# Totals of 31 heads moved from between two VectorE products to behind both, in a decode attention kernel

## The chip, the cores and the metric

The kernel runs on one core of a Trainium2 chip. The metric is device time in microseconds (us), the median of several executions. A profile is one execution recorded by the hardware profiler; its span is about 1.8 us shorter than the device time of the same execution.

Engine names in the profile: PE is TensorE (matmuls), PEld its weight loads, DVE is VectorE, ACT is ScalarE, SP is SyncE, which issues the transfers (DMA).

## The reference

Cut to what matters: one query of 32 heads attends to a cache of 65,536 keys and values per head. A small gated feed-forward part and a sigmoid gate are mixed in.

```
q      = (x @ wq) as 32 heads of 128
scores = q . k_cache / sqrt(128)          # 32 x 65536
p      = softmax(scores)
o      = p . v_cache
a      = o @ wo
b      = (silu(x @ w_gate) * (x @ w_up)) @ w_down
out    = g * a + (1 - g) * b              # g = sigmoid(sum(x * gate_w))
```

The caches are 1.07 GB in bf16, each byte read once. The softmax's division is put off: the kernel forms unnormalised sums, keeps the row sums of the exponentials, and divides at the end by the *totals*.

## The kernel before

A head is two *chunks* of 32,768 keys, so there are 64 chunks, 0 to 63. Three buffers (slots) of the same size hold keys and values in turn. For each chunk VectorE multiplies the keys by the query in place (*product*, two halves per chunk), TensorE sums over each key's 128 elements by matmuls with an identity matrix (*sums*), VectorE finishes the sum (*gather*), ScalarE makes the exponential, and TensorE multiplies by the values (*value product*, 64 matmuls).

```python
def norm(h0, h1):                       # totals
    mms("tot_ps", m_x[...], [(ones, rowsum[:, ...])], ...)       # TensorE
    dve("tot",   ... tensor_reduce(out=tot[:, h0:h1], in_=m_x ...))
    dve("recip", ... reciprocal(tot[:, h0:h1]))

def outputs():                          # normalised outputs of heads 0..30
    dve("oT", ... oT = o_all * tot)

for n in range(N - 1):                  # chunks 0..62
    ...                                 # load keys and values of chunk n
    m = HK if n else EK
    for j in range(0, KPP, m):          # two halves
        block(n, j, m)                  # product on VectorE, sums on TensorE
        if j == 0:
            if c == 0 and h + 1 < H:
                spread(h + 1)
            if pending:
                diagonal()              # TensorE, then ScalarE: last output of a head
            if n == N - 2:              # chunk 62: all of heads 0..30 is done
                norm(0, H - 1)
                outputs()
        while len(todo) > 1:
            gather()
    gather()
    ...
    if n == N - 2:
        turn_outputs(0)                 # t_ps: oT turned by TensorE
    pv(n)                               # value product

# chunk 63, cut: in four quarters, with the last weights
load("v", n, V_END)                     # last values, five pieces
turn_outputs(1)
for i, j in enumerate(range(0, KPP, EK)):
    block(n, j, EK)                     # short product, short sums
    if i == 0:
        rows("b_ps", ...)               # 56 one-column matmuls
        diagonal()
    if i == 1:
        dve("rest", ...)
        rows("a_ps", ...)               # 128 one-column matmuls
    ...
```

The order in which the program issues these calls is the order in which each engine runs them in the profiles: in the kernel before, TensorE runs the first sums of chunk 62 at 2448.51 us, the diagonal at 2457.33 and tot_ps at 2458.30, as issued.

The softmax here doesn't subtract the row's maximum and nothing guards it: scores larger than these inputs give would overflow.

Of the kernel before, what the change touches and what calls it, by code (L numbers as in the profile page):

```python
# [79 lines left out]
def kernel(  # L80
# [18 lines left out]
    _, H, Sk, Dh = A_k_cache.shape  # L99
# [8 lines left out]
    N = H * CH  # L108
# [89 lines left out]
    def load(which, n, pieces):  # L198
        cache = A_k_cache if which == "k" else A_v_cache
        h, c = divmod(n, CH)  # L200
        s = where[which, n] = take()
        src = cache[0, h, c * P * KPP : (c + 1) * P * KPP, :].rearrange(
            "(p j) d -> p j d", j=KPP
        )
        t = view(s, 0, KPP, Dh)
        at = 0
        for m in pieces:
            dma(
                (which, n, at), t[:, at : at + m, :], src[:, at : at + m, :],
                units(s, at * Dh, (at + m) * Dh),  # L210
                sem=f"slot{s}" if len(pieces) == 1 else f"{which}{n}_{at}",
            )
            at += m
        assert at == KPP
# [31 lines left out]
    def mms(key, out_ap, pairs, reads, writes, start=True, stop=True):  # L246


        def fn():
            for i, (a, b) in enumerate(pairs):  # L250
                ins = nc.tensor.matmul(  # L251
                    out_ap, lhsT=a, rhs=b,
                    start=start and i == 0, stop=stop and i == len(pairs) - 1,
                )
            return ins

        op("PE", key, fn, reads, writes)
# [20 lines left out]
    def dve(key, fn, reads, writes):  # L278
        op("DVE", key, fn, reads, writes)
# [26 lines left out]
    def spread(h):  # L306

        act("dq", dq, ident, ACT.Copy, ["ident", "qT"], ["dq"], scale=qT[:, h : h + 1])
        mms("spread", m_sp[:, :Dh], [(ones_b, dq)], ["ones_b", "dq"], ["m_sp"])
        q = h % 2  # L310
        act("q_bc", q_bc[q], m_sp[:, :Dh], ACT.Copy, ["m_sp"], [("q_bc", q)])
# [4 lines left out]
    def block(n, j, m):  # L316

        s, h = where["k", n], n // CH
        qb = q_bc[h % 2]
        q_rep = bass.AP(tensor=qb.tensor, offset=qb.offset, ap=[list(qb.ap[0]), [0, m], [1, Dh]])  # L320
        w = view(s, 0, KPP, Dh)[:, j : j + m, :]
        names = units(s, j * Dh, (j + m) * Dh)
        dve(
            "products", lambda: nc.vector.tensor_tensor(out=w, in0=w, in1=q_rep, op=ALU.mult),  # L324
            names + [("q_bc", h % 2)], names,
        )
        r = ring["S"] % 2
        ring["S"] += 1
        B = 512 // R
        group(  # L330
            ("sums", s, j, m, r),
            [
                (
                    S_ps[r][:, b : b + B, :],
                    [(ident, w[:, b : b + B, i * R : (i + 1) * R]) for i in range(Dh // R)],
                )
                for b in range(0, m, B)
            ],
            names + ["ident"], [("S_ps", r)],
        )  # L340
        todo.append((n, j, m, r))

    def gather():
        n, j, m, r = todo.pop(0)
        b = ring["Sb"] % 2
        ring["Sb"] += 1
        dve(
            "gather",
            lambda: nc.vector.tensor_reduce(  # L349
                out=S_sb[b][:, :m], in_=S_ps[r][:, :m, :], axis=AXIS.X, op=ALU.add  # L350
            ),
            [("S_ps", r)], [("S_sb", b)],
        )
        col = n * RS + j // EK
        act(
            "exp", P_sb[n % 2][:, j : j + m], S_sb[b][:, :m], ACT.Exp,
            [("S_sb", b), "rowsum"], [("P_sb", n % 2, u) for u in range(j // EK, (j + m) // EK)]
            + [("rowsum", col)],
            scale=scale, accum_out=rowsum[:, col : col + 1],
        )  # L360
# [25 lines left out]
    def diagonal():  # L386

        h = pending.pop(0)
        mms(
            ("diagonal", h == H - 1), m_c[:, 0:1],  # L390
            [(O_sb[:, j * Dh : (j + 1) * Dh], pick[:, j : j + 1]) for j in range(VB)],
            ["O_sb", "pick"], ["m_c"], stop=(h < H - 1),
        )
        if h < H - 1:
            act("o_all", o_all[:, h : h + 1], m_c[:, 0:1], ACT.Copy, ["m_c"], [("o_all", h)])

    def hidden():
        parts = []
        for w, wv in enumerate((gate_v, up_v)):
            for ft in range(FT):  # L400
                parts.append(
                    (
                        m_x[:, w * FT + ft : w * FT + ft + 1],
                        [(wv[:, t, bass.ds(ft, P, FT)], Xc[:, t : t + 1]) for t in range(KT)],
                    )
                )
        group("gu", parts, units(0, G0, U0 + KT * F) + ["Xc"], ["m_x"])
        act("gu_sb", gu_sb, m_x[:, : 2 * FT], ACT.Copy, ["m_x"], ["gu_sb"])
        act("eg", eg, gu_sb[:, :FT], ACT.Exp, ["gu_sb"], ["eg"], scale=-1.0)
        dve("eg1", lambda: nc.vector.tensor_scalar_add(eg, eg, 1.0), ["eg"], ["eg"])  # L410
        dve("eg2", lambda: nc.vector.reciprocal(eg, eg), ["eg"], ["eg"])
        dve(
            "eg3",
            lambda: nc.vector.tensor_tensor(out=eg, in0=gu_sb[:, :FT], in1=eg, op=ALU.mult),
            ["eg", "gu_sb"], ["eg"],
        )
        dve(
            "hT",
            lambda: nc.vector.tensor_tensor(out=hT, in0=eg, in1=gu_sb[:, FT:], op=ALU.mult),
            ["eg", "gu_sb"], ["hT"],  # L420
        )

    def gate():
        dve(
            "s_t",
            lambda: nc.vector.tensor_tensor_reduce(
                out=xg, in0=x_row, in1=gw_row, scale=1.0, scalar=0.0,
                op0=ALU.mult, op1=ALU.add, accum_out=s_t,
            ),
            ["x_row", "gw_row"], ["xg", "s_t"],  # L430
        )
        mms("s_ps", m_x[:, 0:1], [(ones[0:1, :], s_t)], ["ones", "s_t"], ["m_x"])
        act("gexp", gval, m_x[:, 0:1], ACT.Exp, ["m_x"], ["gval"], scale=-1.0)
        dve("g1", lambda: nc.vector.tensor_scalar_add(gval, gval, 1.0), ["gval"], ["gval"])
        dve("g2", lambda: nc.vector.reciprocal(gval, gval), ["gval"], ["gval"])
        dve(
            "g3",
            lambda: nc.vector.tensor_scalar(
                out=ngval, in0=gval, scalar1=-1.0, scalar2=1.0, op0=ALU.mult, op1=ALU.add
            ),  # L440
            ["gval"], ["ngval"],
        )
# [15 lines left out]
    def norm(h0, h1):  # L458
        w = CH * RS
        mms("tot_ps", m_x[:, : (h1 - h0) * w], [(ones, rowsum[:, h0 * w : h1 * w])],  # L460
            ["ones", "rowsum"] + [("rowsum", i) for i in range(h0 * w, h1 * w)], ["m_x"])
        dve(
            "tot",
            lambda: nc.vector.tensor_reduce(
                out=tot[:, h0:h1],
                in_=m_x[:, : (h1 - h0) * w].rearrange("p (h c) -> p h c", c=w),
                axis=AXIS.X, op=ALU.add,
            ),
            ["m_x"], [("tot", h0)],
        )  # L470
        dve("recip", lambda: nc.vector.reciprocal(out=tot[:, h0:h1], in_=tot[:, h0:h1]),
            [("tot", h0)], [("tot", h0)])

    def outputs():

        dve(
            "oT",
            lambda: nc.vector.tensor_tensor(
                out=oT[:, : H - 1], in0=o_all[:, : H - 1], in1=tot[:, : H - 1], op=ALU.mult
            ),  # L480
            [("o_all", h) for h in range(H - 1)] + [("tot", 0)], ["oT"],
        )
# [18 lines left out]
    for n in range(N - 1):  # L501
        h, c = divmod(n, CH)
        if c == 0:
            cut[h] = len(plan.ops)
        if n:
            load("k", n, [KPP])
            load("v", n, [KPP])
        m = HK if n else EK
        for j in range(0, KPP, m):
            block(n, j, m)  # L510
            if j == 0:
                if c == 0 and h + 1 < H:
                    spread(h + 1)
                if pending:
                    diagonal()
                if n == N - 2:
                    norm(0, H - 1)
                    outputs()
            while len(todo) > 1:
                gather()  # L520
        gather()
        if n == 0:
            gate()
            hidden()
        if n == N - 2:
            turn_outputs(0)
        pv(n)


    n, h = N - 1, H - 1  # L530
# [132 lines left out]
```

## Time and profile before

| | before |
|---|---|
| median of the first three executions | 2534.17 us (2532.98 to 2534.49) |
| span of the profile | 2530.3 us |
| transfers, share of 16 engines' span | 99.3% |
| VectorE, TensorE busy | 50%, 78% |

The page says what bounds the kernel as a whole. The first line of the fence is the span, the second the mean busy share of the DMA engines in 40 slices of the span (tenths, 9 is 90% or more), the third the queue of the caches (packets, MB, share of 16 engines).

```profile
span 2530.3 us, 19415 instructions
...
DMA  9999999999999999999999999999999999999996
...
q1 hardware_dynamic: 20880, 1087.78, 99.3%
```

Only the last slice is short of full, and the queue is at 99.3% of the span. So in this kernel an engine's wait should cost nothing while it holds up no transfer; that leaves the end. The change sits there, in chunk 62.

This is VectorE's timeline in chunk 62: start, length, the instruction, and in brackets the idle time before it and what ended it.

```profile
2439.76 8.69 DVE L324 TENSOR_TENSOR slot_67<-slot_67,q_bc_79 128x16384 bf16<-128x16384 bf16 x1 [12.39 <-DMA slot_67<-in_A_k_cache_dram]
2458.96 0.42 DVE L464 TENSOR_REDUCE tot<-m_x 128x31 f32<-128x248 f32 x1 [10.50 <-PE m_x L251]
2459.41 0.35 DVE L471 RECIPROCAL tot<-tot 128x31 f32<-128x31 f32 x1
2459.86 0.20 DVE L478 TENSOR_TENSOR oT<-o_all,tot 128x31 bf16<-128x31 f32 x1
2459.97 8.68 DVE L324 TENSOR_TENSOR slot_67<-slot_67,q_bc_79 128x16384 bf16<-128x16384 bf16 x1
```

The first product (8.69 us) starts when the keys land at 2439.76. Then VectorE stands idle 10.50 us for one TensorE result, tot_ps in `m_x`, works 0.97 us on totals, and only then starts the second product. The keys of the second product came with those of the first. Why tot_ps comes late is seen in the chain of waits (the work that ended last, followed back; start, length, engine and what it writes: `S_ps` are sums, `m_c` with x8 the diagonal, `m_x` at x2 tot_ps and at x56 a group of one-column matmuls called b_ps, `O_ps` the value product).

```profile
2448.51 8.81 PE S_ps_101 L265 x32
2457.33 0.98 PE m_c L251 x8
2458.30 0.63 PE m_x L251 x2
...
2460.06 8.61 DVE slot_67 L324
...
2468.71 8.97 PE S_ps_102 L265 x32
...
2479.41 13.97 PE O_ps L251 x64
...
2493.58 3.56 PE S_ps_101 L265 x16
2497.14 1.83 PE m_x L265 x56
2498.97 0.98 PE m_c L251 x8
2499.95 5.21 PE S_ps_102 L265 x16
```

tot_ps (`m_x` at 2458.30) stands on TensorE behind the first sums (8.81 us) and the diagonal (0.98 us). From the value product at 2479.41 on, the chain is TensorE without a gap until its last products. Two short sums of equal work take 3.56 and 5.21 us. That difference is the clock (1.00 during the first; 0.59 on average over 2500 to 2504 us). Groups at half clock are called *cold*, stretches at half clock *slow spells*.

Last, the transfers at the end: windows of 2 us, with TensorE's granted clock (1.00 is full speed, 0.50 half), the DMA share and GB/s as the last three columns.

```profile
2490.00:2492.00 2.00, 2.00 (x11) 0.82 (x10) 0.00 (x0) 0.00 (x0) 0.00 (x0) 1.00 0.31 131
2492.00:2494.00 2.00, 2.00 (x14) 0.77 (x13) 0.00 (x0) 0.57 (x2) 0.00 (x0) 1.00 0.00 0
2494.00:2496.00 2.00, 2.00 (x11) 0.94 (x10) 0.00 (x0) 0.09 (x2) 0.00 (x0) 1.00 0.87 262
```

There is a hole in the transfers: the last values need the slot that the value product of chunk 62 reads, so they are issued only when it ends, at 2493.42.

### The profile page before, as it was taken

How to read it: one execution, taken by the hardware profiler on the slowest of the kernel's cores; microseconds unless marked ns; L12 is line 12 of the kernel's file. 1: busy time of each engine (PE TensorE's matmuls, PEld its weight loads, DVE VectorE, ACT ScalarE, POOL GpSimd, SP SyncE). 2: the span in 40 equal slices, each digit the busy share in tenths (PEclk: the TensorE clock that was granted, in tenths of full speed). 3: DMA queues.
4: the chain of work that ended last, by engine and by line, in shares of the span. 5: the costliest groups of instructions: out<-in, count | busy, mean ns of one | idle time of the engine just before them, and what ended most of it. 6: DMA issues, size and time to landing. Idle time of an engine off the chain costs nothing.

```text
span 2530.3 us, 19415 instructions
## 1 busy us (share of the span) xinstructions
PE 1981.2 (78%) x9115; PEld 823.6 (33%) x9115; DVE 1268.3 (50%) x286; ACT 97.4 (4%) x398; POOL 1.9 (0%) x9
## 2 busy tenths in 40 slices
PE   4787877877877878778778778787787787787868
PEld 2233332333333333323333333333333233333324
DVE  3455355464464554554644645545546446455453
ACT  0000000000000000000000000000000000000000
POOL 0000000000000000000000000000000000000000
PEclk8888988989889889889989898898898998988988
DMA  9999999999999999999999999999999999999996
GB/s 421 432 433 433 435 434 434 434 432 436 434 434 435 431 437 433 435 435 431 436 433 436 435 431 435 434 434 436 432 435 434 433 436 433 435 433 434 434 430 289
DMA packets 20906, 1088.09 MB, mean 430 GB/s; under 512 B 2450, under 2 KB 2580, under 8 KB 2836
## 3 DMA queue, kind: packets, MB, share of 16 engines
q1 hardware_dynamic: 20880, 1087.78, 99.3%
q8 instruction: 16, 0.26, 0.0%
q14 instruction: 6, 0.05, 0.0%
q10 hardware_dynamic: 4, 0.00, 0.0%
HBM read 1087.77 MB, written 0.00 MB: 430 GB/s over the span
## 4 chain that ended last, share of the span: by engine, by line
DMA 44%; PE 41%; DVE 13%; ACT 1%; another core or an unknown queue 0%; issue 0%; SPq 0%; DVEq 0%; ACTq 0%
PE O_ps L251 18%; DMA slot_67<-in_A_k_cache_dram 16%; DMA slot_66<-in_A_k_cache_dram 14%; DMA slot_65<-in_A_k_cache_dram 14%; PE S_ps_101 L265 12%; PE S_ps_102 L265 9%; DVE slot_67 L324 4%; DVE slot_66 L324 4%; DVE slot_65 L324 3%; DVE S_sb_82 L349 2%; PE m_c L251 1%; PE m_x L265 1%; ACT P_sb_83 L274 1%; DMA slot_65<-in_A_wq_dram 0%
## 5 line engine op out<-in xcount | busy, mean ns | idle before, releaser
L265 PE MATMUL S_ps_101<-slot_67,ident 128*128 128x512 bf16 x704 | 204.6, 462 | 133.7 <-DVE slot_67 L324 133.7
L265 PE MATMUL S_ps_101<-slot_66,ident 128*128 128x512 bf16 x672 | 195.5, 463 | 127.9 <-DVE slot_66 L324 127.9
L265 PE MATMUL S_ps_101<-slot_65,ident 128*128 128x512 bf16 x672 | 190.1, 453 | 133.8 <-DVE slot_65 L324 133.8
L349 DVE TENSOR_REDUCE S_sb_82<-S_ps_102 128x128 f32<-128x1024 f32 (+1 forms) x66 | 78.7, 1192 | 396.9 <-PE S_ps_102 L265 396.9
L324 DVE TENSOR_TENSOR slot_67<-slot_67,q_bc_79 128x16384 bf16<-128x16384 bf16 (+1 forms) x26 | 207.9, 8031 | 133.1 <-DMA slot_67<-in_A_k_cache_dram 133.1
L324 DVE TENSOR_TENSOR slot_65<-slot_65,q_bc_78 128x16384 bf16<-128x16384 bf16 x22 | 190.2, 8689 | 146.5 <-DMA slot_65<-in_A_k_cache_dram 146.5
L324 DVE TENSOR_TENSOR slot_66<-slot_66,q_bc_78 128x16384 bf16<-128x16384 bf16 (+1 forms) x24 | 190.6, 7977 | 136.9 <-DMA slot_66<-in_A_k_cache_dram 121.2
L324 DVE TENSOR_TENSOR slot_67<-slot_67,q_bc_78 128x16384 bf16<-128x16384 bf16 x20 | 172.9, 8688 | 120.6 <-DMA slot_67<-in_A_k_cache_dram 120.6
L324 DVE TENSOR_TENSOR slot_65<-slot_65,q_bc_79 128x16384 bf16<-128x16384 bf16 x20 | 172.9, 8688 | 119.1 <-DMA slot_65<-in_A_k_cache_dram 119.1
L324 DVE TENSOR_TENSOR slot_66<-slot_66,q_bc_79 128x16384 bf16<-128x16384 bf16 x20 | 172.9, 8689 | 117.7 <-DMA slot_66<-in_A_k_cache_dram 117.7
L251 PE MATMUL O_ps<-slot_67,P_sb_83 128*4 128x512 bf16 x704 | 155.6, 382 | 28.5 <-ACT P_sb_83 L274 18.3
L251 PE MATMUL O_ps<-slot_65,P_sb_83 128*4 128x512 bf16 x704 | 153.7, 379 | 19.9 <-ACT P_sb_83 L274 19.9
L251 PE MATMUL O_ps<-slot_66,P_sb_84 128*4 128x512 bf16 x704 | 153.7, 379 | 19.3 <-ACT P_sb_84 L274 19.3
L265 PE MATMUL S_ps_102<-slot_67,ident 128*128 128x512 bf16 x704 | 159.4, 385 | 9.9 <-DVE slot_67 L324 9.8
L265 PEld LDWEIGHTS S_ps_101<-slot_67,ident 128*128 128x128 bf16 x704 | 79.0, 115 | 258.7 <-DVE slot_67 L324 144.3
L265 PEld LDWEIGHTS S_ps_101<-slot_66,ident 128*128 128x128 bf16 x672 | 75.7, 115 | 247.7 <-DVE slot_66 L324 138.7
L265 PEld LDWEIGHTS S_ps_101<-slot_65,ident 128*128 128x128 bf16 x672 | 74.3, 113 | 249.9 <-DVE slot_65 L324 144.4
L251 PE MATMUL O_ps<-slot_67,P_sb_84 128*4 128x512 bf16 x640 | 139.7, 379 | 18.3 <-ACT P_sb_84 L274 18.3
L251 PE MATMUL O_ps<-slot_65,P_sb_84 128*4 128x512 bf16 x640 | 139.7, 379 | 18.3 <-ACT P_sb_84 L274 18.3
L251 PE MATMUL O_ps<-slot_66,P_sb_83 128*4 128x512 bf16 x640 | 139.7, 379 | 17.5 <-ACT P_sb_83 L274 17.5
L265 PE MATMUL S_ps_102<-slot_66,ident 128*128 128x512 bf16 x672 | 148.8, 379 | 1.3 <-DVE slot_66 L324 1.3
L265 PE MATMUL S_ps_102<-slot_65,ident 128*128 128x512 bf16 x672 | 148.6, 379 | 0.3 <-DVE slot_65 L324 0.2
(83 smaller groups left out, 860.6 us busy)
## 6 DMA issues: line engine op xcount, KB each, us to landing
slot_66<-in_A_k_cache_dram SPq DMA_DIRECT2D x4, 2048.0 KB, 24.9
slot_67<-in_A_k_cache_dram SPq DMA_DIRECT2D x4, 2048.0 KB, 17.8
slot_65<-in_A_wq_dram SPq DMA_DIRECT2D x1, 4096.0 KB, 12.4
slot_66<-in_A_wo_dram SPq DMA_DIRECT2D x1, 4096.0 KB, 30.8
slot_65<-in_A_v_cache_dram SPq DMA_DIRECT2D x1, 4096.0 KB, 13.3
slot_65<-in_A_v_cache_dram SPq DMA_DIRECT2D x1, 2048.0 KB, 17.8
slot_65<-in_B_w_gate_dram SPq DMA_DIRECT2D x1, 1792.0 KB, 35.0
slot_65<-in_B_w_up_dram SPq DMA_DIRECT2D x1, 1792.0 KB, 38.8
```

The costliest lines, as they stand in the source:

```text
L251: ins = nc.tensor.matmul(out_ap, lhsT=a, rhs=b, start=start and i == 0, stop=stop and i == len(pairs) - 1,)
L265: ins = nc.tensor.matmul(out_ap, lhsT=a, rhs=b, start=(i == 0), stop=(i == len(pairs) - 1))
L274: "ACT", key, lambda: nc.scalar.activation(out=out_ap, in_=in_ap, func=func, **kw),
L324: "products", lambda: nc.vector.tensor_tensor(out=w, in0=w, in1=q_rep, op=ALU.mult),
L349: lambda: nc.vector.tensor_reduce(out=S_sb[b][:, :m], in_=S_ps[r][:, :m, :], axis=AXIS.X, op=ALU.add),
```

## The change

The intent is to let the two products of chunk 62 follow each other as in every other chunk. The totals are issued behind the second half's product and sums instead of between the halves.

```diff
                 if pending:
                     diagonal()
-                if n == N - 2:
-                    norm(0, H - 1)
-                    outputs()
+            elif n == N - 2:
+                norm(0, H - 1)
+                outputs()
             while len(todo) > 1:
                 gather()
```

No instruction is added or removed. On TensorE, tot_ps moves behind the second sums; on VectorE, three small instructions move behind the second product, ahead of the two gathers.

## The prediction

> **What bounds the kernel now.** DMA, almost everywhere: 430 GB/s over the span, 99% of 16 engines (page, parts 2 and 3). A chunk of keys and values takes 38.6 us, which the transfers fill, so the change can only act at the end. There (windows of 4 us) the DMA share is about 1.0 until 2488 us, falls to 0.59 and 0.43 in 2488-2496, and is full again until 2513. The chain of waits of the last 90 us has no DMA in it: product, sums, tot_ps, totals, product, sums, gather, exponent, value product (64 matmuls, from 2479.41), then unbroken TensorE work until 2525.1.
>
> **What the change moves.** Nothing is added or removed. In the last chunk but one (keys landed 2439.76) the first product ends at 2448.45. The totals need tot_ps, which stands on TensorE behind sums 1 (8.8 us, partly at the slow clock) and the diagonal (1.0 us). VectorE runs its queue in order ([...]the trace agrees), so it idles 10.50 us until 2458.96, spends 0.42 + 0.35 + 0.20 us on totals, reciprocal and oT, and starts the second product only at 2459.97. Without that wait the second product starts at 2448.5 and ends at 2457.2 (earlier chunks: two products in 17.29 us).
>
> **New sequence (estimate from those durations).** Sums 1 to 2457.3, diagonal to 2458.3, sums 2 without a wait at the fast clock (7.08 us in the chunks before) to 2465.4, tot_ps to 2466.0. VectorE waits for it some 8.8 us in place of 10.5, but only the two gathers are behind it. Totals to 2467.0, two gathers of 1.22 us, exponent; gather start to value product is 1.71 us before. Value product from 2469.95 instead of 2479.41: 9.4 us earlier.
>
> **Does it pass to the end?** Behind the value product TensorE is the chain. Its needs: the first last-chunk key piece lands at 2478.2 (bound by the queue of transfers, unchanged), so its product ends at 2482.7, before sums want it at 2484.2. Later pieces landed by 2490.6. The value slot is free 9.4 us earlier, so the last values are issued at 2484 rather than 2493.42, with keys still in the queue: the DMA hole of some 4 to 5 us closes and the last piece lands near 2511 instead of 2516.3; TensorE wants it after about 2514. So nearly all 9.4 us reach the end.
>
> **Loss.** TensorE idles about 4 us before the value product, broken by two tiny matmul groups. Before, gaps of 1.8 us left it fast and gaps of 4.8 us or more made the next matmuls 0.43 us apart instead of 0.22. [...] I charge 0.5 to 0.8 us.
>
> **Predicted:** 2534.2 - 9.4 + 0.6 = about 2525.3 us, 80% range 2522.8 to 2528.6. Faster by over 2%: 0.01; within 2%: 0.98; slower: 0.01.
>
> **What would show it.** The timeline: the two products of that chunk back to back (17.3 us); the VectorE wait for tot_ps 8 to 9 us, now behind both; the value product near 2470; the second pair of last key pieces issued near 2465.5 and the values near 2484; no DMA hole at 2488-2496; the stretch from value product start to the last result still 45.7 us.
>
> **What would make it wrong.** The value product at the slow clock for more than 4 us; the last values or keys landing later than estimated, so that TensorE waits for DMA in the last chunk; another clock in the last chunk's short sums (5.2 us slow, 3.5 fast).

The sum came to "about 2525.3 us". Its +0.6 stands for the charge of 0.5 to 0.8 us, which was the author's guess between two cases of the trace: no loss behind a gap of 1.75 us (value product of 13.97 us at 2427.86) and a loss behind one of 4.85 us (sums of 9.38 us at 2409.83, where the next took 7.07).

## The result, and the profile after

| | before | after |
|---|---|---|
| median | 2533.57 us (4 executions, 2531.68 to 2534.49) | 2522.31 us (4 executions, 2521.99 to 2522.57) |
| span of the profile | 2530.3 us | 2520.2 us |
| mean granted clock | 0.902 | 0.905 |

The ratio is 0.9956, 95% interval 0.9939 to 0.9974. A ratio is the mean time of one kernel's executions over that of the other's of the same rounds, so it is not quite the ratio of the two medians. By the 2% limit the two kernels are the same; the difference itself is clear of noise. The result lies 0.5 us below the predicted range and 3.0 us below its centre.

VectorE in chunk 62, after:

```profile
2439.53 17.30 DVE L324 TENSOR_TENSOR slot_67<-slot_67,q_bc_79 128x16384 bf16<-128x16384 bf16 x2 [12.33 <-DMA slot_67<-in_A_k_cache_dram]
2465.60 0.42 DVE L464 TENSOR_REDUCE tot<-m_x 128x31 f32<-128x248 f32 x1 [8.78 <-PE m_x L251]
2466.05 0.35 DVE L471 RECIPROCAL tot<-tot 128x31 f32<-128x31 f32 x1
...
2466.61 1.22 DVE L349 TENSOR_REDUCE S_sb_81<-S_ps_101 128x128 f32<-128x1024 f32 x1
```

Both products are one line of 17.30 us. The wait for tot_ps is still there, 8.78 us, but behind it stand only the gathers. The chain of waits after:

```profile
2448.28 8.87 PE S_ps_101 L265 x32
2457.15 0.98 PE m_c L251 x8
2458.13 7.01 PE S_ps_102 L265 x32
2465.14 0.43 PE m_x L251 x2
...
2469.45 15.43 PE O_ps L251 x64
...
2485.07 3.56 PE S_ps_101 L265 x16
2488.63 1.84 PE m_x L265 x56
2490.47 0.98 PE m_c L251 x8
2491.44 3.56 PE S_ps_102 L265 x16
```

Three things differ from before. The value product starts at 2469.45 instead of 2479.41. It takes 15.43 us instead of 13.97, because its first matmuls ran at half clock (0.50 from 2469.0 to 2472.4 us: its first seven matmuls started about 0.43 us apart, the later ones 0.22). And the second short sums take 3.56 us instead of 5.21. The hole in the transfers is gone:

```profile
2490.00:2492.00 2.00, 2.00 (x25) 1.65 (x24) 1.49 (x3) 0.35 (x2) 0.00 (x0) 1.00 1.24 532
2492.00:2494.00 2.00, 2.00 (x11) 0.89 (x10) 2.00 (x1) 0.00 (x0) 0.00 (x0) 1.00 0.83 352
```

**The sum of the two profiles.** The last VectorE instruction starts at 2525.80 before and at 2515.65 after, 10.15 us earlier. Measured from the landing of chunk 62's keys, which came 0.23 us earlier after, this is:

| term | predicted | measured |
|---|---|---|
| keys of chunk 62 land earlier | 0 | -0.23 |
| landing to value product (39.65 us before, 29.92 after) | -9.46 | -9.73 |
| length of the value product | +0.6 | +1.46 |
| second short sums of chunk 63 | 0 | -1.65 |
| sum | -8.86 | -10.15 |

So the move itself was predicted to 0.3 us. What was not predicted is a clock term, and that the medians differ by 11.3 us where the profiles' executions (2532.06 and 2521.99 us) differ by 10.1.

### The profile page after: what moved, and what is told of

It is laid out like the page before. It is cut to its first block, busy times and chain, and to the rows that moved or that the text cites. A ratio compares the mean times of both kernels' runs of the same rounds, so it can differ in the third digit from the quotient of the medians. Undisturbed runs are those within 1.5% of the kernel's fastest.

```text
span 2520.2 us, 19415 instructions
## 1 busy us (share of the span) xinstructions
PE 1979.0 (79%) x9115; PEld 823.1 (33%) x9115; DVE 1268.4 (50%) x286; ACT 97.4 (4%) x398; POOL 1.9 (0%) x9
## 4 chain that ended last, share of the span: by engine, by line
DMA 44%; PE 41%; DVE 13%; ACT 1%; another core or an unknown queue 0%; issue 0%; SPq 0%; DVEq 0%; ACTq 0%
PE O_ps L251 18%; DMA slot_67<-in_A_k_cache_dram 16%; DMA slot_66<-in_A_k_cache_dram 14%; DMA slot_65<-in_A_k_cache_dram 14%; PE S_ps_101 L265 12%; PE S_ps_102 L265 9%; DVE slot_66 L324 4%; DVE slot_67 L324 4%; DVE slot_65 L324 3%; DVE S_sb_82 L349 2%; PE m_c L251 2%; PE m_x L265 1%; ACT P_sb_83 L274 1%; DMA slot_65<-in_A_wq_dram 0%
```

## The experiments

**Theory 1** (the mechanism): the gain is VectorE's wait for tot_ps taken out of TensorE's chain, and it reaches the end because TensorE is that chain. *Rivals*: VectorE work between the products spoils them whatever it waits for; or the gain came from the transfers, since the last values are issued earlier.

**Theory A** (the miss): the unpredicted part is the phase of TensorE's clock, that is, where single groups of matmuls fall against the moments at which the clock changes, together with a baseline taken from few executions. *Rival, theory B*: it lies in the transfers, that is, in when the keys land.

For theory A each profile was also read in windows of half a microsecond from 2440 to 2516 us, to work out from the clock column when the slow spells begin and end. In all 18 the spells that both began and ended there were about 3.41, 6.83, 10.24 or 13.65 us long (shift_before has 10.24, 13.65 and 3.42), that is, multiples of 3.41 us.

### Both kernels again

No edit.

> The kernel before, unaltered, for its spread and a second profile. Theory A (the unpredicted gain is the clock phase of single stretches, and the baseline median was taken from few runs): ratio to the kernel before 1.000 within 0.0005; its single times spread over 1.5 to 3 us again, and in the new profile the stretch from the last keys' landing of the last chunk but one to the end (90.6 us in the first profile, 2439.76 to 2530.3) differs by the cold and warm lengths of single TensorE groups (short sums 3.6 or 5.2 us). Theory B (the spread lies in the transfers): that stretch is the same within 0.3 us and only the landing moves.

> The changed kernel, unaltered. Both theories: 10 to 12 us under the kernel before (ratio 0.9953 to 0.9961), spread under 1 us. Theory A: the stretch from the last keys' landing of the last chunk but one to the end is 80.7 us as in the first profile unless a TensorE group falls on the other side of a clock change; the second short sums of the last chunk may be 5.2 us again in place of 3.56 us. Theory B: the stretch is fixed.

Measured: before_rep 2532.01 us, ratio to the kernel before 1.000 (0.9986 to 1.0013), executions from 2531.27 to 2534.54. after_rep 2521.96 us, ratio 0.9958 (0.9945 to 0.9972), from 2520.95 to 2522.95. From the start of chunk 62's first product to the last VectorE instruction the profiles have 86.04 and 86.15 us before, 76.12 and 75.57 us after. The second short sums of after_rep took 3.56 us again, the value product 15.36 us. The gain is repeated, about 10.2 us by these four profiles, and the clock terms of the pair repeat as well: they are not a freak of one execution.

### tot_ps first: TensorE's order changed, the totals left between the products

Against the kernel before; `oT` alone goes behind both products, as in the change.

```diff
+        if n == N - 2:
+            norm_ps(0, H - 1)               # tot_ps ahead of the first sums
         for j in range(0, KPP, m):
             block(n, j, m)
             if j == 0:
                 ...
                 if n == N - 2:
-                    norm(0, H - 1)
-                    outputs()
+                    norm(0, H - 1, ps=False) # totals stay between the products
+            elif n == N - 2:
+                outputs()
```

> The kernel before with tot_ps alone moved on TensorE ahead of the first sums of the last chunk but one; totals and reciprocal stay on VectorE between the two products, oT goes behind both. Theory 1 (the cost was the wait of VectorE for tot_ps, not 0.8 us of its own work there): as fast as the change or faster; value product at 2466.9 in place of 2469.45 and at the full clock; then the first product of the last chunk (keys land 2477.9, product 4.4 us) holds TensorE up for about 1.4 us, so 2.0 to 3.5 us below the change, about 2519.5 us. Rival (any VectorE work between the products spoils their pairing): stays near the kernel before, 2530 or more.

Measured: 2521.55 us (2520.59 to 2522.24), ratio 0.9956 (0.9942 to 0.9969), against 2521.96 us for after_rep on the same chip. VectorE's timeline in chunk 62:

```profile
2439.54 8.69 DVE L324 TENSOR_TENSOR slot<-slot,q_bc 128x16384 bf16<-128x16384 bf16 x1 [12.32 <-DMA slot<-in_A_k_cache_dram]
2448.15 0.41 DVE L469 TENSOR_REDUCE tot<-m_x 128x31 f32<-128x248 f32 x1
2448.59 0.35 DVE L476 RECIPROCAL tot<-tot 128x31 f32<-128x31 f32 x1
2448.86 8.63 DVE L324 TENSOR_TENSOR slot<-slot,q_bc 128x16384 bf16<-128x16384 bf16 x1
```

The totals and the reciprocal (0.76 us) still stand between the products, without a wait, and the whole gain is there. So the cost before was the wait for TensorE and not the work; the first rival is out. The value product ended at 2480.8 and not at 2484.9, as expected, but the 2.0 to 3.5 us below the change did not come. The chain of waits shows where they went:

```profile
2477.97 4.44 DVE slot L324
...
2482.45 3.63 PE S_ps L265 x16
2486.08 1.84 PE m_x L265 x56
2487.91 0.98 PE m_c L251 x8
2488.89 5.25 PE S_ps L265 x16
```

TensorE waited 1.4 us for the first product of chunk 63, whose keys land at 2477.9 whatever is done (that was in the expectation). Then the second short sums ran cold, 5.25 us against 3.56 in the change, and the third and fourth took 9.35 us together against 8.61. The clock terms gave back 2.4 us.

### The change with TensorE kept busy before the value product

```diff
         if n == N - 2:
             turn_outputs(0)
+            filler("fill", 10)   # 10 needless 128x512 matmuls, result unread
```

> The changed kernel with 10 needless 128x512 matmuls (2.2 us at full clock, into a bank nobody reads then) in TensorE's gap before the value product. Theory A (the value product's first 7 matmuls ran at half clock because the gap let the clock drop; cost 15.43 - 13.97 = 1.46 us): value product back to 13.97 us, time 1.0 to 1.5 us below the change. Rival (the 1.46 us is hidden by the wait for the last chunk's keys and values, or the clock drops all the same): no change within 0.4 us.

Measured: 2522.58 us (2521.91 to 2524.37), against 2521.96 us for after_rep on the same chip. The chain of waits of its profile:

```profile
2470.40 13.97 PE O_ps L251 x64
...
2484.56 3.56 PE S_ps L265 x16
...
2490.93 5.25 PE S_ps L265 x16
```

The value product is back at 13.97 us, as theory A says, so the idle gap did cost 1.46 us there. (The eight profiles with the change's order up to there and no filler, whose slow spells lie at various times, have 15.36 to 16.93 us.) But the second short sums ran cold and took 1.69 us more, and nothing was won. Here the changes of the clock also lay elsewhere (a slow spell began at 2446.7 instead of 2445.1), so the run does not say that the filler alone made the short sums cold. It says that a saving of 1.46 us in this chain was lost to the clock again 6.6 us behind the value product, where the second short sums took 1.69 us more.

### The last values issued later

```diff
-    load("v", n, V_END)
     turn_outputs(1)
     ...
             dve("rest", ...)
+            load("v", n, V_END, ["rest"])                   # late_a
+            load("v", n, V_END, [("S_ps", todo[-1][3])])    # late_b, instead
```

> The changed kernel with the last values issued later on purpose: only when VectorE has made 'rest' (2490.7 instead of 2484.9, 5.8 us later). Theory 1 (what reached the end is TensorE's chain; the earlier issue of the values only has to be early enough): the queue still holds keys until 2492.5, so no transfer is later and the time is that of the change within 0.5 us. Rival (the gain came from issuing the last values 9 us earlier, so that more than half of it goes when they are issued 5.8 us later): 5 us slower or more.

> The same, values issued only after the second short sums of the last chunk (about 2495.0, 10 us later than in the change). Theory 1: a hole of 4 to 5 us opens in the transfers, the last piece lands about 2516.5 to 2518, TensorE then waits for values in its last products: 2 to 4 us slower than the change, so even then more than half of the change's gain stays. Rival: 9 us or more slower, all the gain gone.

Measured: 2527.33 us (ratio 0.9980) and 2538.94 us (ratio 1.0025), by the numbers nearer to the rival. The profile of late_a shows that the edit made a wait of its own:

```profile
DVE rest L553 <- DMA slot<-in_A_v_cache_dram: 13.3, 1, 13.3
```

VectorE's next write of `rest` waited 13.3 us for the values. The transfers had been entered as readers of `rest`, so its next writer had to wait until they had landed; in late_b the same happened to the sums. These two runs say nothing on either theory. They were mended by letting only the issue wait:

```diff
+        for r in after:
+            plan.readers[r] = plan.readers[r][: -len(pieces)]
```

> late_a mended: there the transfers of the values counted as readers of 'rest', so VectorE's next write of it waited 13.3 us for them, a wait that the edit itself made. Here only the issue waits. Values issued at about 2491 instead of 2484.9; the queue ran empty near 2490.4, so packets start near 2493 and the last piece lands at about 2514.7 instead of 2512. Theory 1 (TensorE's chain is what reached the end, the values have 2 to 3 us to spare): the change within 0.7 us. Rival (the gain is the earlier issue of the values): about 6 us slower, the 5.8 us passed on.

> late_b mended in the same way. Values issued at about 2495.5, 10.6 us later than in the change and about 2 us later than the kernel before issues them; last piece lands near 2519 and TensorE's last products wait for it. Theory 1: end set by that landing, 4 to 5 us slower than the change, so 6 us of its gain remain although the values come later than in the kernel before. Rival: as slow as the kernel before or slower (2532 or more).

Measured: late_a2 2523.98 us (2522.71 to 2524.43), ratio 0.9966 (0.9953 to 0.9980); late_b2 2526.91 us (2525.61 to 2528.32), ratio 0.9978 (0.9965 to 0.9992); the kernel before was 2531.86 us on that chip. Against the change (2522.0 to 2522.3 us on other chips) late_a2 is 2 us slower, more than the 0.7 expected, and not the rival's 6: its values were issued at 2492.0, and the last products waited 1.2 us for them; the remainder is its first sums of 9.67 us where the change has 8.87. In late_b2 the chain runs through the values:

```profile
2499.80 21.13 DMA slot<-in_A_v_cache_dram
...
2520.97 0.60 PE m_c L253 x16
```

They were issued from 2497.9 on, 4.5 us later than the kernel before issues them, and still the kernel is 5 us faster than the kernel before. So the earlier issue of the values is not where the gain came from. It is a condition of keeping all of it: issued 7.1 us later (late_a2) they cost 1.2 us. One more transfer moved with the change: the second pair of the last key pieces is issued at 2465.17 instead of 2477.70. No run delayed it alone; but in the kernel before no transfer stands in the chain of waits after 2439.76, so it was not what held that kernel up.

### One-column groups ahead of the short sums

```diff
+    rows("b_ps", wd, ...)
+    diagonal()
     for i, j in enumerate(range(0, KPP, EK)):
         block(n, j, EK)
-        if i == 0:
-            rows("b_ps", wd, ...)
-            diagonal()
```

This edit alone on the change, and together with tot_first ("both"):

> The changed kernel with b_ps and the diagonal (one-column matmuls, 1.84 + 0.98 us) moved on TensorE from behind the last chunk's first short sums to ahead of them. No wait is there to be filled, so TensorE's order alone changes. Theory A (one-column groups let the clock drop for the group behind them): the second short sums no longer stand behind such a group and take 3.56 us, the first may take 5.2 us instead; within 1.7 us of the change either way. Rival (the place of these groups is of no account): same within 0.4 us and no group's length changes.

> tot_ps first (as in tot_first) together with b_ps and the diagonal ahead of the last chunk's first short sums. In tot_first TensorE stood idle 1.5 us for the first product of the last chunk (2482.4) and its second short sums ran cold (5.25 us). Theory: the two groups fill that wait; first sums start at 2483.8 and second sums run at full clock: 2.5 to 3.3 us below tot_first, about 2518.6 us, near what the last values' landing (2511) allows. Rival (the end is already held by transfers, not by TensorE): as tot_first within 0.7 us.

Measured: after_bfirst 2523.98 us, spread wide from 2521.16 to 2527.47, ratio 0.9969 (0.9956 to 0.9983). both 2521.40 us (2519.54 to 2523.05), ratio 0.9953 (0.9940 to 0.9967). In after_bfirst's profile the first and second short sums took 7.01 us together, so neither ran cold, yet the median is no better than the change; why two of five executions reached 2527.4 us is not known. In both's profile:

```profile
2481.83 1.96 PE m_x L265 x56
2483.79 1.39 PE m_c L251 x8
2485.18 9.90 PE S_ps L265 x32
```

The two groups did fill the wait, but the clock fell to 0.50 during them, at 2484.2, and the first two short sums took 9.90 us instead of 3.63 + 5.25 in tot_first. The expected 2.5 to 3.3 us did not come; the median is within 0.2 us of tot_first's, on another chip. No version tried is clearly faster than the change.

### The start pushed against the clock

```diff
+    op("DVE", "delay", lambda: nc.vector.memset(slot[0][:, :4096], 0.0), writes=units(0, 0, 4096))
     dma("wq", wq_sb, ...)
```

The end of a window at 2445.1 to 2445.2, of which the expectation speaks, is a fall of the clock that the profiles show: at 2445.1 to 2445.2 in before, before_rep, after, after_rep and tot_first, at 2446.7 in after_warm.

> The kernel before with a needless memset on VectorE ahead of the first weight load, which pushes everything behind by about 1.7 us against the windows of the clock (in five of six profiles a window ended at 2445.1 to 2445.2 us). Theory A: besides the push, single groups change length: the first sums of the last chunk but one from 8.8 to about 9.7 us, the second from 9.0 to about 9.4; time = before + push + about 1.2 us. Theory B (lengths do not depend on the phase): before + push, every group as long as before within 0.2 us.

> The changed kernel with the same push of about 1.7 us. Theory A: first sums of the last chunk but one about 9.7 us instead of 8.8, the value product anything from 13.97 to 15.7 us, and a short sum of the last chunk 5.2 us instead of 3.6 or the reverse; so change + push + 1 to 3 us, and the difference to shift_before is not the 10.1 us of the first pair of profiles but 1 us or more off it. Theory B: change + push, all lengths as in the change, difference to shift_before 10 us.

Measured: shift_before 2533.89 us (2533.53 to 2534.90), shift_after 2524.72 us (2523.69 to 2526.26), with 2533.13 us for the kernel before on that chip. The keys of chunk 62 landed 2.1 to 2.3 us later than without the push. In shift_before's profile the first sums took 9.86 us and the second 9.50, as theory A expected; but the third and fourth short sums took 6.93 us together instead of 8.6, so the end came only about 1.5 us later. In shift_after the first sums took 9.00 us and not 9.7. Theory B's fixed lengths are refuted, but theory A's sizes were only half right: the clock's changes do not stay at a fixed time from the start (without any push, the end of one slow spell lay between 2451.2 and 2453.8 in six profiles, see the next table), so a push at the start did not set the phase. The runs were of less use than hoped.

### Four more profiles of the kernel before

These were to learn why executions of the kernel before scatter to 2534.5 us. No edit.

> The kernel before, unaltered, for one more profile. Theory A: if this execution is a slow one (2533.5 us or more), its extra 1.5 to 2.5 us over the two profiles at hand (2531.8 and 2532.1) lie in the lengths of TensorE groups after 2439 us and its clock windows end at another time than 2445.2. Theory B: they lie in a later landing of the keys of the last chunk but one (2439.6 to 2439.8 so far).

> As for the run before it: stretch from landing to end 86.0 to 86.2 us if the clock window ends at 2445.2, longer by 1 us or more if the window's end is elsewhere and the execution slow (theory A); landing moved (theory B).

> As for the run before it: stretch from landing to end 86.0 to 86.2 us if the clock window ends at 2445.2, longer by 1 us or more if the window's end is elsewhere and the execution slow (theory A); landing moved (theory B).

> As for the run before it: stretch from landing to end 86.0 to 86.2 us if the clock window ends at 2445.2, longer by 1 us or more if the window's end is elsewhere and the execution slow (theory A); landing moved (theory B).

None of the four was a slow one: 2532.17, 2530.94, 2532.56 and 2531.34 us. They still decide between A and B within the ordinary range. The slow spell here is the one that runs into chunk 62's first sums.

| profile | keys used at | slow spell ends | first sums | landing to last VectorE instruction | span |
|---|---|---|---|---|---|
| before_f | 2439.49 | 2451.2 | 8.53 | 85.59 | 2529.6 |
| before_rep | 2439.57 | 2452.0 | 8.88 | 86.15 | 2530.0 |
| before | 2439.76 | 2452.1 | 8.81 | 86.04 | 2530.3 |
| before_c | 2439.71 | 2452.5 | 9.07 | 86.45 | 2530.4 |
| before_e | 2439.70 | 2453.1 | 9.34 | 86.85 | 2530.7 |
| before_d | 2439.49 | 2453.8 | 9.80 | 85.54 | 2529.2 |

First sums of chunk 62, and third and fourth short sums of chunk 63 (a line of 32 matmuls each), from the chains of waits of before_f and then of before_d:

```profile
2448.24 8.53 PE S_ps L265 x32
...
2508.67 8.61 PE S_ps L265 x32
```

```profile
2448.23 9.80 PE S_ps L265 x32
...
2510.64 6.93 PE S_ps L265 x32
```

The start of chunk 62 varies by 0.3 us, the stretch behind it by 1.3 us and the span by 1.5. The first sums get longer by half of what the slow spell's end moves, 1.27 us for 2.57 us, as fits matmuls at half clock (in the first sums of before 0.43 us from one to the next until the clock rose at 2452.1, 0.22 behind it). before_d has the longest first sums and yet the shortest stretch, because its third and fourth short sums both ran at the full clock (6.93 us). So within these six, theory A holds and B does not.

For the executions at 2534 us there is no profile. Without the four executions of the result, 46 executions of the unaltered kernel before were made in this study beside the experiments (none of them slow in state; five single ones unknown): their median is 2532.3 us and five of them are above 2534 us. The mean granted clock of those five is 0.901, that of the ones under 2533 us 0.903. That fits the clock, but no trace shows it; this part stays open.

## Why the prediction was right or wrong

- **What bounds the kernel, and the wait: right.** Transfers fill 99%; only the end can be moved; the second product was held by the wait for tot_ps. tot_first shows that it was the wait and not the work, of which it leaves 0.76 of the 0.97 us in place.
- **VectorE still waits 8 to 9 us, now behind both products: right** (8.78 us). The prediction took VectorE's queue to run in order. The trace of the kernel before agrees: three instructions of 0.97 us, with a product behind them whose keys had landed, cost 10.50 us of waiting.
- **Value product 9.4 us earlier: right.** It was 9.73 us from the landing of the keys. tot_ps took 0.43 us of chain rather than 0.63 there, and the two gathers overlapped slightly.
- **It passes to the end: right.** TensorE's chain is unbroken in both profiles, and late_b2 keeps 5 us of gain with values issued later than in the kernel before. One detail was misread: "landed by 2490.6" took the median landing time of two key pieces, 12.5 us, for that of the last one. It made no difference.
- **Values issued at 2484, no hole in the transfers: right** (2484.9).
- **Loss at the slow clock, "I charge 0.5 to 0.8 us": too small.** The charge was a guess. It measured 1.46 us in the profile after and 1.39 in after_rep. That error alone would have made the kernel slower than predicted.
- **The failed step is the sum: "2534.2 - 9.4 + 0.6 = about 2525.3 us".** Two of its terms were mis-sized. First, the base. 2534.2 was the median of three executions, while every duration was read from an execution of 2532.06 us; the median of 46 further executions is 2532.3. That is 1.9 us of the 3.0 by which the centre was off. Second, a term was missing that the prediction had itself named as a danger: "another clock in the last chunk's short sums (5.2 us slow, 3.5 fast)" was entered as zero. It measured -1.65 us. With the value product's +0.86 beyond the charge, and -0.5 from an earlier landing and start, the profiles' sum comes to 1.3 us below the predicted one. (1.9 and 1.3 exceed 3.0 by 0.2: 2532.3 less the profiles' 10.15 is 2522.15, and the measured median is 2522.31.) How the 3.0 us divide depends on the base: against the four executions of the result (2533.57) the base has 0.6 us of it and the gain 2.4, of which the two profiles show 1.3.
- **The range was too narrow.** Its lower edge left 2.5 us under the centre. The base's own spread (2531 to 2534.5 us) and one group of the clock (1.65 us) are together larger.

**Why the second short sums ran cold before and not after.** Between the first and the second short sums stand b_ps and the diagonal, one-column matmuls, 2.8 us. In windows of 4 us the kernel before shows TensorE busy throughout (the first number behind the window's length) while the clock, third column from the end, falls:

```profile
2496.00:2500.00 4.00, 4.00 (x71) 3.40 (x69) 0.99 (x3) 0.14 (x1) 0.00 (x0) 0.98 1.03 442
2500.00:2504.00 4.00, 4.00 (x12) 1.44 (x12) 4.00 (x1) 0.21 (x2) 0.00 (x0) 0.59 1.10 471
```

How the clock moved is read from the clock column of the profiles alone, in the same windows of half a microsecond. In each of the 18 profiles all its changes between 2440 and 2516 us lie whole numbers of steps of 3.413 us (a third of 10.24) from one another, within 0.02 us; in the kernel before they are at 2445.23, 2452.06, 2462.30, 2472.54, 2499.85, 2503.26, 2510.09 and 2513.50. In the kernel before, the step from 2496.43 to 2499.85 took in 2.70 of the 2.82 us of b_ps and the diagonal (modelled starts and ends of the chain of waits); the clock was 1.00 up to its end and 0.50 from there, so the second short sums ran cold. In the kernel after, a step's edge at 2489.49 cut the two groups into 0.86 and 1.96 us, and the clock stayed at 1.00. The same for nine profiles:

| profile | most of b_ps and the diagonal in one step | clock behind it | second short sums |
|---|---|---|---|
| after_warm | 2.82 us | 0.50 | 5.25 us |
| tot_first | 2.80 us | 0.50 | 5.25 us |
| shift_before | 2.82 us | 0.50 | 5.25 us |
| before | 2.70 us | 0.50 | 5.21 us |
| late_b2 | 2.40 us | 0.50 | 4.95 us |
| after_rep | 2.02 us | 1.00 | 3.56 us |
| after | 1.96 us | 1.00 | 3.56 us |
| shift_after | 1.88 us | 1.00 | 3.56 us |
| late_a2 | 1.44 us | 1.00 | 3.56 us |

Others fit: before_rep and before_c to before_f have 2.54 to 2.81 us and ran cold (5.08 to 5.25 us), late_b 1.51 us and did not (3.57 us); with the two groups moved ahead, the clock fell behind 2.35 us (both) and not behind 1.70 us (after_bfirst). late_a is left out, because its chain leaves TensorE in between. No threshold follows: of the 128 one-column matmuls of a_ps 2.26 us lay in one step in before_d (from 2508.38) and the clock stayed at 1.00, and 2.20 us in tot_first (from 2492.93) and it fell. The change moved the two groups by about 8.5 us, two and a half steps. In all seven profiles with the order of the kernel before they ran into the drop; in six of the seven with the change's order and no filler they did not. No run set the phase at will, so this is a coincidence read from traces and not shown by an edit; what makes the clock change is not shown, and why the edge lay so in nearly every execution stays open. That the gain of 1.65 us has nothing to do with the totals follows from tot_first, which has all of the mechanism and does not have it.

## What to carry to other kernels

Put an instruction that waits for another engine behind those that could already run: here three instructions of 0.97 us, waiting 10.50 us, held up a ready product of 8.68 us, and moving either end of the wait (the waiter later, or what it waits for earlier) cured it equally here (2522.0 and 2521.6 us). Near the end of a TensorE chain an expected gain under about 2 us should carry the clock as a term with its own spread, not as zero, since the second short sums, which stand between one-column matmuls, took 3.56 us in some of these profiles and 5.25 us in others. And take the base of a prediction from the execution whose durations are used, or from many executions; a median of three was off by 1.9 us here, about a sixth of the whole gain.
